# Useless TensorE products that stay on through the first attention block, three normalisations moved to POOL, and new costs for the weight splitting

## The chip, the cores and the metric

One core of one Trainium2 chip runs the whole program in one launch. The metric is device time in microseconds (us). Three runs of the kernel before took 1007.84, 1008.41 and 1009.18 us, so their median is 1008.41 us. Engines: PE (TensorE) multiplies matrices, DVE (VectorE), ACT (ScalarE) and POOL (GpSimd) work on elements, SP issues the DMAs.

## The reference, cut to what matters

```python
# attention: 4 x 8 heads x 768 tokens, head size 64, in windows of a chunk, its context and 8 memory tokens
scores = scale * np.matmul(q_c, k_full.transpose(0, 1, 3, 2))
a = np.exp(scores - np.max(scores, axis=-1, keepdims=True))
a = a / (np.sum(a, axis=-1, keepdims=True) + 1e-09)
out[:, :, c_start:c_end] = np.matmul(a, v_full)
...
# dense layer on 3072 tokens x 512
h = x @ w_in                                  # 512 -> 2048
x = np.maximum(0.01 * h, h) @ w_out           # 2048 -> 512
...
# 8 experts: each token goes to one, by the largest gate values, 384 tokens an expert
out[mask] = np.maximum(x[mask] @ w1[e], 0.0) @ w2[e]
```

## The kernel before

Work is cut into 32 groups of 96 queries (n in the code). Four groups make one block of 384 tokens (j); the dense layer then goes over a block in 16 steps (f), each with 128 columns of the hidden layer. Every product of the dense layer is made of three fp32r products, since each weight and each activation is held as a high and a low part (winh and winl, wouth and woutl, x1h and x1l, gh and gl).

A group of attention passes five stations. `scores` (L818) multiplies queries and keys into two PSUM banks; DVE takes scores, mask and row maximum (L822); ACT takes the exponentials (L827). `normalise` makes the reciprocal sums on DVE (L843, L845) and multiplies the 96x1024 exponentials by them (L847). `transpose` turns them on PE in two halves (L863), each into its own bank, and two copies bring them to SBUF as AT (L852 on ACT or L854 on DVE). `mix` multiplies by the values (L886) into one bank; that bank gives x1h (a cast on ACT or DVE) and x1l (a subtraction on DVE, L892).

The weights of the dense layer arrive as 64-bit numbers in 32 chunks, two for each step f (an input chunk and an output chunk). `weights` loads a chunk (L902, four buffers), scales its upper words on ACT (L909), puts the fp32 bits together on DVE in three passes (L910, L911, L913), casts the high part on ACT or POOL (L916, L917) and subtracts it on POOL for the low part (L918). This goes on beside the first block of the dense layer, until all chunks are split. `gemm1` (L934) and `gemm2` (L1027) of step f cannot start before their chunk.

The first block has no dense layer beside it. Its groups use other banks: the transposes of the first four groups go into po0 and po1, the mixed values into po2, which later gather `gemm2`; scores of the groups 1 and 3 use the two banks ph of `gemm1`.

The order of the instructions on each engine is set by a planner (`Plan`). Every piece of work is an `op` with the engines it may run on and a cost in us for each, a key and its dependencies; the planner plays through time with these costs and writes the instruction when it comes up. An engine runs its instructions in that order. A changed cost so moves work in later places too.

`keep_warm` plans a chain of useless products with the lowest priority: `warm` multiplies the identity by itself into columns 384 to 511 of a bank in the list `spots`, if one of them has not yet been taken over by later work; else it writes nothing. Nobody reads these columns. Before, the list holds the first buffer of po2 and one bank of the first group's scores.

Of the kernel before, what the change touches and what calls it, by code (L numbers as in the profile page):

```python
# [688 lines left out]
def kernel(ctx, tc, q, k, v, w, w_gate_t, we, out):  # L689
# [22 lines left out]
    S6 = SL * NF - ND  # L712
    EARLY = (S6 - 97.5) / 12
    PRE = 19
    NWARM, PAUSE, COLD = 60, 0.2, 8

    ctx.enter_context(tc.manual_schedule())
    P = Plan(nc)
# [83 lines left out]
    def scores(n):  # L802
        a = A[n]
        g = n % GB
        var = 0 if g == 0 else (2 if g == GB - 1 else 1)
        r = r_h if n < APB and n % 2 else r_a
        ps = [r.take() for _ in range(2)]
        X, st = a["X"], a["st"] = (r_ws if n == 2 else r_X).take(), r_st.take()
        if n == 2:
            X.view = lambda t: (t[:QB].rearrange("p a b -> p (a b)").bitcast(FT)  # L810
                                .rearrange("p (a b) -> p a b", a=H))
        a["e"] = []

        def mm():
            for i in range(KD):
                for r in range(2):
                    p = slice(64 * r, 64 * r + 64)
                    nc.tensor.matmul(ps[r].t[:QB, i * 128:(i + 1) * 128], a["q"][1]()[p, i, :], a["k"][1]()[p, i, :],  # L818
                                     start=True, stop=True)

        def mx(h):
            V.tensor_tensor_reduce(out=X.t[:, h, :], in0=ps[h % 2].t[:QB, h // 2 * 128:h // 2 * 128 + 128],  # L822
                                   in1=masks[:, var, :], scale=-scale, scalar=3.0e38, op0=OP.add, op1=OP.min,
                                   accum_out=st.t[:, 0, h:h + 1])

        def ex(h):
            S.activation(X.t[:, h, :], X.t[:, h, :], AF.Exp, bias=st.t[:, 0, h:h + 1], scale=-1.0,  # L827
                         accum_out=st.t[:, 2, h:h + 1])

        if n == 0:  # L830
            spots.append(ps[1])
        t = P.op(("T", 0.95), mm, [a["qd"], a["kd"]], [*ps, a["q"][0], a["k"][0]])
        for r in range(2):
            hs = slice(r, H, 2)
            for h in range(H)[hs]:
                o = P.op(("V", 0.215), lambda h=h: mx(h), [t], [ps[h % 2], X, st])
                a["e"].append(P.op(("S", 0.387), lambda h=h: ex(h), [o], [X, st]))

    def normalise(n):
        a = A[n]  # L840
        X, st = a["X"], a["st"]

        o = P.op(("V", 0.12), lambda: V.tensor_scalar(st.t[:, 3, :], st.t[:, 2, :], 1e-9, None, op0=OP.add),  # L843
                 [a["e"]], [st])
        o = P.op(("V", 0.12), lambda: V.reciprocal(st.t[:, 3, :], st.t[:, 3, :]), [o], [st])  # L845
        a["n"] = P.op({"V": 1.14} if n >= N1 or n < APB else {"V": 1.7, "G": 2.1},
                      lambda e=V if n >= N1 or n < APB else G: e.tensor_tensor(  # L847
            X.t, X.t, st.t[:, 3, :, None].to_broadcast([QB, H, 128]), op=OP.mult), [o], [X, st])

    def copy(e, out, x):  # L850
# [5 lines left out]
    def transpose(n):  # L856
        a = A[n]
        AT = a["AT"] = r_AT.take()
        a["t"] = []

        def tr(p, hh):
            for i in range(KD):
                nc.tensor.transpose(p.t[:, i * QB:(i + 1) * QB], a["X"].t[:, 4 * hh + i, :], ident[:QB, :QB])  # L863

        for hh in range(2):
            p = (r_o[hh] if n < APB else r_a).take()
            o = P.op(("T", 0.35), lambda p=p, hh=hh: tr(p, hh), [a["n"]], [p, a["X"]])
            a["t"].append(P.op({"S": 0.38, "V": 0.47} if n < APB else {"S": 0.38}, lambda e=S, p=p, hh=hh: copy(
                e, AT.t[:, 4 * hh:4 * hh + 4, :], p.t[:, :KD * QB].rearrange("p (a b) -> p a b", a=KD)),
                [o], [p, AT]))  # L870
# [3 lines left out]
    def mix(n):  # L874
        a = A.pop(n)
        j, u = divmod(n, APB)
        if u == 0:
            X1[j] = [r.take() for r in r_x1], []
        p = (r_o[2] if n < APB else r_a).take()
        sl = slice(u * QB, (u + 1) * QB)  # L880
        hi, lo = X1[j][0]

        def mm(hh):
            for h in range(4 * hh, 4 * hh + 4):
                i, r = divmod(h, 2)
                nc.tensor.matmul(p.t[64 * r:64 * r + 64, i * QB:(i + 1) * QB], a["v"].t[:, h, :], a["AT"].t[:, h, :],  # L886
                                 start=True, stop=True)

        pv = lambda: p.t[:, :KD * QB].rearrange("p (a b) -> p a b", a=KD)
        o = P.op(("T", 0.83), lambda: [mm(0), mm(1)], [a["t"], a["vd"]], [p, a["v"], a["AT"]])  # L890
        x = P.op({"S": 0.38, "V": 0.47} if n < APB else {"S": 0.38}, lambda e=S: copy(e, hi.t[:, :, sl], pv()), [o], [p, hi])
        y = P.op(("V", 0.47), lambda: V.tensor_tensor(lo.t[:, :, sl], pv(), hi.t[:, :, sl].bitcast(FT),  # L892
                                                      op=OP.subtract), [x], [p, hi, lo])
        X1[j][1].extend([x, y])
# [4 lines left out]
    def weights(c):  # L899
        f, half = divmod(c, 2)  # L900
        s, a, m, b = (r.take() for r in (r_ws, r_wa, r_wm, r_wp))
        d = P.dma(1.46, lambda: nc.sync.dma_start(s.t.rearrange("p a b -> p (a b)"),  # L902
                                                  w64[f][:, half * 1024:(half + 1) * 1024]), [], [s])

        hi, lo = (x[:, f, :] for x in (win if half == 0 else wout))
        mm = lambda: a.t.bitcast(FT)

        mi, lw, hw = (lambda: m.t.bitcast(I32)), (lambda: s.t[:, :, 0]), (lambda: s.t[:, :, 1])
        o = P.op(("S", 0.57), lambda: S.activation(m.t, hw().bitcast(FT), AF.Copy, scale=2.0 ** -112), [d], [s, m])  # L909
        o = P.op(("V", 0.45), lambda: V.tensor_scalar(b.t, mi(), 3, None, op0=OP.logical_shift_left), [o], [b, m])  # L910
        o = P.op(("V", 0.62), lambda: V.scalar_tensor_tensor(  # L911
            b.t, hw(), -0x80000000, b.t, op0=OP.bitwise_and, op1=OP.bitwise_or), [o], [s, b])
        o = P.op(("V", 0.62), lambda: V.scalar_tensor_tensor(  # L913
            a.t, lw(), 29, b.t, op0=OP.logical_shift_right, op1=OP.bitwise_or), [o], [s, a, b])
        x = P.op({"G": 0.7, "S": 0.54}, lambda e: (
            G.tensor_scalar(hi, mm(), 1.0, 0.0, op0=OP.mult, op1=OP.add) if e is G  # L916
            else S.activation(hi, mm(), AF.Copy)), [o], [a])  # L917
        y = P.op({"G": 1.3}, lambda e=G: e.tensor_tensor(lo, mm(), hi.bitcast(FT), op=OP.subtract),  # L918
                 [x], [a])
        WD[c] = [x, y]  # L920
# [156 lines left out]
            P.dep(o, [last], lat=pause if n > COLD else 0.0)  # L1077

    def warm():
        b = next((b for b in spots if not b.gone), None)  # L1080
        if b:
            nc.tensor.matmul(b.t[:, 384:], ident, ident, start=True, stop=True)

# [179 lines left out]
```

## Time and profile before

| what | us |
|---|---|
| median of three runs | 1008.41 |
| the profiled execution, its own time | 1008.72 |
| its span, first to last instruction | 1007.0 |
| PE busy in the span | 982.5 |
| DVE busy | 770.6 |
| ACT busy | 441.6 |
| POOL busy | 134.8 |

A line of the timeline gives the start, the duration, the engine, the line of the kernel, what is written from what, and the count; in brackets stands how long the engine had been idle and what it waited for. Matmuls overlap in the pipeline, so the distance from one start to the next is the better measure of what a group costs. The windows view gives the busy time of an engine in a stretch and the TensorE clock that was granted, as a share of 2.4 GHz: 1.00 is 2.4 GHz, 0.50 is 1.2 GHz.

### The profile page before, as it was taken

To read this page: it belongs to the slowest core of one execution; us is meant where nothing else is said; L and a number is where in the kernel's file an instruction comes from. 1 tells how busy PE (TensorE), PEld (TensorE's weight loads), DVE (VectorE), ACT (ScalarE), POOL (GpSimd) and SP (SyncE) were. 2 spreads that over 40 slices of the span, in tenths; PEclk is the share of its full clock that TensorE was granted. 3 is DMA by queue.
4 is the path that set the end of the run, shared out by engine and by line. 5 is a ranking of instruction groups with operands and counts; after the bars stand their busy time and mean duration, and the time that the engine had idled before them with its cause. 6 is when DMAs were issued, how large, how long until landed. Compare 5 with 4: busy or idle time off the path is not lost.

```text
span 1007.0 us, 17270 instructions
## 1 busy us (share of the span) xinstructions
PE 982.5 (98%) x6040; PEld 856.7 (85%) x6040; DVE 770.6 (77%) x2573; ACT 441.6 (44%) x1183; POOL 134.8 (13%) x149
## 2 busy tenths in 40 slices
PE   7999999999999999999999999999999999999997
PEld 6877888888988888888888889778888888888996
DVE  7989799698698599689689494588977888875720
ACT  7766634444444443544444324023434334334521
POOL 0767521000000000000000000010021112111211
PEclk9889999999999999999999999999999999999999
DMA  8656520021012111111210000044442624526600
GB/s 279 209 189 208 177 88 29 30 71 48 29 62 58 29 62 46 42 61 30 58 61 12 1 1 27 16 128 161 131 163 100 199 106 146 170 72 201 228 32 31
DMA packets 36326, 95.48 MB, mean 95 GB/s; under 512 B 4368, under 2 KB 8464, under 8 KB 36112
## 3 DMA queue, kind: packets, MB, share of 16 engines
q1 hardware_dynamic: 32400, 81.80, 25.3%
q0 software_dynamic: 3840, 12.59, 3.7%
q8 instruction: 47, 0.77, 0.3%
q14 instruction: 39, 0.32, 0.1%
HBM read 81.79 MB, written 12.58 MB: 94 GB/s over the span
## 4 chain that ended last, share of the span: by engine, by line
PE 81%; DVE 6%; issue 4%; DMA 3%; ACT 3%; POOL 2%; POOLq 0%; ACTq 0%; DVEq 0%; SPq 0%
PE po L1027 23%; PE ph L934 23%; PE ph L610 13%; PE po L633 11%; PE pa L818 2%; PE pa L886 2%; DVE junk L1057 2%; DMA wst<-in_w_dram 2%; PE pa L863 2%; PE pc L312 2%; ACT X L827 1%; DMA wgb<-in_w_gate_t_dram 1%; PE pt L479 1%; DVE wa L913 1%; DVE wp L911 1%
## 5 line engine op out<-in xcount | busy, mean ns | idle before, releaser
L1057 DVE CUSTOM_DVE_ANT_0 junk<-x,wgb 128x512 bf16<-128x512 f32 x296 | 207.8, 702 | 5.9 <-DMA wgb<-in_w_gate_t_dram 1.2
L942 ACT ACTIVATE gs<-ph 128x384 f32<-128x384 f32 x128 | 62.6, 489 | 195.2 <-PE ph L934 188.2
L1027 PE MATMUL po<-woutl,gh 128*128 128x512 f32 x336 | 134.5, 400 | 3.4 <-POOL woutl L918 3.4
L1027 PE MATMUL po<-wouth,gh 128*128 128x512 f32 x336 | 136.9, 407 | 0.0
L943 DVE TENSOR_TENSOR gs<-ph,gs 128x384 f32<-128x384 f32 x128 | 71.0, 555 | 85.0 <-ACT gs L942 84.5
L1027 PE MATMUL po<-wouth,gl 128*128 128x512 f32 x336 | 132.8, 398 | 1.2 <-POOL gl L945 1.2
L827 ACT ACTIVATE X<-X,st 96x128 f32<-96x128 f32 x248 | 97.0, 393 | 49.2 <-DVE st L822 49.0
L934 PE MATMUL ph<-x1h,winh 128*128 128x384 f32 x512 | 112.6, 342 | 1.2 <-ACT x1h L852 0.9
L934 PE MATMUL ph<-x1h,winl 128*128 128x384 f32 x512 | 111.0, 338 | 0.0
L934 PE MATMUL ph<-x1l,winh 128*128 128x384 f32 x512 | 110.3, 336 | 0.0
L934 PEld LDWEIGHTS ph<-x1h,winh 128*128 128x128 f32 x512 | 92.7, 190 | 11.6 <-POOL winh L916 1.2
L616 ACT ACTIVATE egh<-ph 128x384 fp32r<-128x384 f32 x64 | 31.4, 491 | 155.1 <-PE ph L610 151.0
L934 PEld LDWEIGHTS ph<-x1h,winl 128*128 128x128 f32 x512 | 93.0, 189 | 1.0
L934 PEld LDWEIGHTS ph<-x1l,winh 128*128 128x128 f32 x512 | 91.2, 189 | 0.3
L1027 PEld LDWEIGHTS po<-wouth,gl 128*128 128x128 f32 x336 | 63.4, 189 | 15.7 <-POOL gl L945 2.1
L1027 PEld LDWEIGHTS po<-woutl,gh 128*128 128x128 f32 x336 | 63.6, 189 | 14.9 <-POOL woutl L918 4.7
L1027 PEld LDWEIGHTS po<-wouth,gh 128*128 128x128 f32 x336 | 63.4, 189 | 13.9 <-ACT wouth L917 0.2
L944 ACT ACTIVATE gh<-gs 128x384 fp32r<-128x384 f32 x112 | 58.7, 524 | 36.5 <-DVE gs L943 36.3
L617 DVE SCALAR_TENSOR_TENSOR egl<-ph,egh 128x384 fp32r<-128x384 f32 x64 | 35.3, 552 | 45.1 <-ACT egh L616 44.8
L822 DVE CUSTOM_DVE_ANT_0 X<-pa,masks 96x128 f32<-96x128 f32 x232 | 56.7, 280 | 4.1 <-PE pa L818 4.1
L1142 POOL IOTA ij<- 128x128 int32 x1 | 0.2, 234 | 425.8 <-DVE L L1057 425.8
L945 DVE TENSOR_TENSOR gl<-gs,gh 128x384 fp32r<-128x384 f32 x88 | 48.5, 551 | 10.2 <-ACT gh L944 10.1
(243 smaller groups left out, 1932.0 us busy)
## 6 DMA issues: line engine op xcount, KB each, us to landing
west<-in_we_dram SPq DMA_DIRECT2D x56, 512.0 KB, 4.5
wst<-in_w_dram SPq DMA_DIRECT2D x32, 512.0 KB, 4.3
kt<-in_k_dram SPq DMA_DIRECT2D x31, 256.0 KB, 3.5
vt<-in_v_dram SPq DMA_DIRECT2D x30, 256.0 KB, 2.7
qt<-in_q_dram SPq DMA_DIRECT2D x31, 192.0 KB, 3.2
x2d<-x SPq DMA_DIRECT2D x21, 256.0 KB, 2.8
x<-in_we_dram SPq DMA_DIRECT2D x16, 256.0 KB, 3.0
wgb<-in_w_gate_t_dram SPq DMA_DIRECT2D x1, 2048.0 KB, 8.3
```

What stands on the lines that cost most here:

```text
L610: nc.tensor.matmul(ph.t[:, :TB], w[a].t[:, k * 128:(k + 1) * 128], xs[x].t[:, k, :], start=(n == 0), stop=(n == 3 * KD - 1))
L617: b = P.op(("V", 0.47), lambda: V.scalar_tensor_tensor(gl.t, ph.t[:, :TB], 0.0, gh.t.bitcast(FT), op0=OP.max, op1=OP.subtract), [a], [ph, ...
L633: nc.tensor.matmul(ACC[p][i].t, l.t[:, 128 * i:128 * i + 128], w[a].t[:, 512:1024], start=(f == 0 and n == 0), stop=(f == NF - 1 and n == 2))
L822: V.tensor_tensor_reduce(out=X.t[:, h, :], in0=ps[h % 2].t[:QB, h // 2 * 128:h // 2 * 128 + 128], in1=masks[:, var, :], scale=-scale, scal ...
L827: S.activation(X.t[:, h, :], X.t[:, h, :], AF.Exp, bias=st.t[:, 0, h:h + 1], scale=-1.0, accum_out=st.t[:, 2, h:h + 1])
L934: nc.tensor.matmul(ph.t[:, :TB], win[wt][:, f, kk * 128:(kk + 1) * 128], xt.t[:, kk, :], start=(n == 0 and kk == 0), stop=(n == 2 and kk = ...
L942: o = P.op(("S", 0.37), lambda: S.activation(t.t, ph.t[:, :TB], AF.Copy, scale=0.01), [o], [ph, t], key=k)
L943: o = P.op(("V", 0.47), lambda: V.tensor_tensor(t.t, ph.t[:, :TB], t.t, op=OP.max), [o], [ph, t], key=k)
L944: x = P.op(("S", 0.42), lambda: S.activation(gh(), t.t, AF.Copy), [o, gd], [t, *gb], key=k)
L945: y = P.op({"V": 0.47} if j > 1 else {"V": 0.47, "G": 0.96} if j else {"G": 0.96}, lambda e=V if j > 1 else G: e.tensor_tensor(gl(), t.t, ...
L1027: nc.tensor.matmul(acc.t, lt()[:, sl], wout[wt][:, f, :], start=(f == 0 and n == 0), stop=(n == 2 and (f == NF - 1 or s == S6 - 1)), skip_ ...
L1057: V.tensor_tensor_reduce(out=pools["wgb"].tile([128, DM], BF, name="junk"), in0=x, in1=WGB[0][:, e, :], scale=1.0, scalar=0.0, op0=OP.mult ...
```

## The change

It has three parts. The useless products may now go into the banks of the first four groups' transposes and mixed values, always the latest one that is in use, and up to 110 of them are planned where 60 were. The normalisation (L847) of the groups 0, 1 and 2 goes to POOL; that of group 3 stays on DVE. The planner's costs for the three bit passes on DVE and for the normalisations are raised.

```diff
-    NWARM, PAUSE, COLD = 60, 0.2, 8
+    NWARM, PAUSE, COLD = 110, 0.2, 8
...
-        if n == 0:
-            spots.append(ps[1])
...
-        a["n"] = P.op({"V": 1.14} if n >= N1 or n < APB else {"V": 1.7, "G": 2.1},
-                      lambda e=V if n >= N1 or n < APB else G: e.tensor_tensor(
+        eng = {"V": 1.2} if n >= N1 or n == APB - 1 else {"G": 2.1} if n < APB - 1 else {"V": 1.8, "G": 2.1}
+        a["n"] = P.op(eng, lambda e=V if n >= N1 or n == APB - 1 else G: e.tensor_tensor(
             X.t, X.t, st.t[:, 3, :, None].to_broadcast([QB, H, 128]), op=OP.mult), [o], [X, st])
...
             p = (r_o[hh] if n < APB else r_a).take()
+            if n < APB:
+                spots.append(p)
...
         p = (r_o[2] if n < APB else r_a).take()
+        if n < APB:
+            spots.append(p)
...
-        o = P.op(("V", 0.45), lambda: V.tensor_scalar(b.t, mi(), 3, None, op0=OP.logical_shift_left), [o], [b, m])
-        o = P.op(("V", 0.62), lambda: V.scalar_tensor_tensor(
+        o = P.op(("V", 0.62), lambda: V.tensor_scalar(b.t, mi(), 3, None, op0=OP.logical_shift_left), [o], [b, m])
+        o = P.op(("V", 0.64), lambda: V.scalar_tensor_tensor(
             b.t, hw(), -0x80000000, b.t, op0=OP.bitwise_and, op1=OP.bitwise_or), [o], [s, b])
-        o = P.op(("V", 0.62), lambda: V.scalar_tensor_tensor(
+        o = P.op(("V", 0.64), lambda: V.scalar_tensor_tensor(
             a.t, lw(), 29, b.t, op0=OP.logical_shift_right, op1=OP.bitwise_or), [o], [s, a, b])
...
-        b = next((b for b in spots if not b.gone), None)
+        b = next((b for b in spots[::-1] if (b.tile or b is spots[0]) and not b.gone), None)
```

Lines from L830 on stand up to two lower or higher in the changed file (L886 becomes L888, L934 L936, L1082 L1084, L847 L845, L918 L920).

PE, from the second half of group 1's transposes to the transposes of group 2. The names po with a number are buffers of the banks po0 to po2; in brackets stands the engine for whose earlier instruction a row waits. Before:

```order
L886 MATMUL po_346<-AT,vt 64x96 [waits DMAHW5_49,DVE_49,Activation_49]
L886 MATMUL po_346<-AT,vt 64x96 x3
L886 MATMUL po_346<-AT,vt 64x96 [waits Activation_49]
L886 MATMUL po_346<-AT,vt 64x96 x3
L863 MATMUL po_361<-ident,wst 128x96 [waits DVE_49,PE_49]
```

The same place now:

```order
L1084 MATMUL po_333<-ident 128x128 x2
L1084 MATMUL po_333<-ident 128x128 [waits Activation_49]
L888 MATMUL po_352<-AT,vt 64x96 [waits DMAHW5_49,DVE_49,PE_49]
L888 MATMUL po_352<-AT,vt 64x96 x7
L1084 MATMUL po_352<-ident 128x128
L1084 MATMUL po_352<-ident 128x128 [waits DVE_49]
L1084 MATMUL po_352<-ident 128x128
L1084 MATMUL po_352<-ident 128x128 [waits DVE_49]
L861 MATMUL po_387<-ident,wst 128x96 [waits PE_49,Pool_49]
```

Seven useless products now stand around the mix of group 1. Three of them wait: the first for ACT's copy of the bank po_333, the two others for DVE's cast and for DVE's subtraction from po_352. In turn these copies wait for the product ahead of them in the same bank.

PE, from the mix of group 3 to the first product of `gemm1`, now (before, `gemm1` followed the mix directly, and its third part waited for DVE):

```order
L888 MATMUL po_453<-AT,vt 64x96 x7
L1084 MATMUL po_453<-ident 128x128
L1084 MATMUL po_453<-ident 128x128 [waits DVE_49]
L1084 MATMUL po_453<-ident 128x128 x2
L1084 MATMUL po_453<-ident 128x128 [waits DVE_49]
L936 MATMUL ph<-x1h,winh 128x384 [waits Activation_49]
L936 MATMUL ph<-x1h,winh 128x384 x3
L936 MATMUL ph<-x1h,winl 128x384 [waits Pool_49]
```

The last product waits for DVE's subtraction x1l of group 3, and `gemm1` stands behind it. Five more products follow between the first steps of `gemm1`; 45 are written in all, where 21 were.

POOL, from its start of real work. Before:

```order
L916 TENSOR_SCALAR winh<-wa 128x512
L918 TENSOR_TENSOR winl<-wa,winh 128x512
L916 TENSOR_SCALAR winh<-wa 128x512
L918 TENSOR_TENSOR winl<-wa,winh 128x512
L918 TENSOR_TENSOR woutl<-wa,wouth 128x512
L916 TENSOR_SCALAR winh<-wa 128x512
L918 TENSOR_TENSOR winl<-wa,winh 128x512
L945 TENSOR_TENSOR gl<-gs,gh 128x384 x2
```

Now:

```order
L845 TENSOR_TENSOR X<-X,st 96x1024 x2
L845 TENSOR_TENSOR wst<-wst,st 96x1024
L920 TENSOR_TENSOR winl<-wa,winh 128x512 x2
L947 TENSOR_TENSOR gl<-gs,gh 128x384
L920 TENSOR_TENSOR woutl<-wa,wouth 128x512
L918 TENSOR_SCALAR winh<-wa 128x512
L920 TENSOR_TENSOR winl<-wa,winh 128x512
L947 TENSOR_TENSOR gl<-gs,gh 128x384
```

The three normalisations stand first on POOL, and the casts of the first two input chunks have left it (they are on ACT). On DVE the three normalisations of 96x1024 are gone from the first block; two copies AT and three casts x1h that ACT had done stand there now, and the first three bit passes come after them. In the attention that follows, the transposes and the mix of a group stand up to one step f earlier on PE than before; the routing and expert stages have the same work in a slightly other order.

## Rows read from the trace of the kernel before

**Rows 1.** The page: span, and PE busy us (share) and instructions.
```profile
span 1007.0 us, 17270 instructions
...
PE 982.5 (98%) x6040; PEld 856.7 (85%) x6040; DVE 770.6 (77%) x2573; ACT 441.6 (44%) x1183; POOL 134.8 (13%) x149
```
**Rows 2.** Windows, PE alone: stretch, length, PE busy (x), granted clock, DMA share, GB/s.
```profile
20.00:24.00 4.00, 1.04 (x17) 0.93 0.84 277
...
60.00:64.00 4.00, 4.00 (x21) 0.50 0.76 230
...
96.00:100.00 4.00, 2.39 (x14) 1.00 0.51 166
```
**Rows 3.** Timeline of PE, end of the first block and first steps of gemm1.
```profile
21.28 0.97 PE L886 MATMUL po<-AT,ve 128*64 128x96 f32 x16 [1.21 <-ACT X L827]
25.04 1.51 PE L863 MATMUL po<-ident,X 96*128 96x96 f32 x8 [2.79 <-DVE X L847]
...
28.93 1.62 PE L934 MATMUL ph<-x1h,winh 128*128 128x384 f32 x4 [0.89 <-ACT x1h L852]
...
33.98 0.85 PE L934 MATMUL ph<-x1h,winl 128*128 128x384 f32 x4
34.67 0.85 PE L934 MATMUL ph<-x1l,winh 128*128 128x384 f32 x4
```
**Rows 4.** Timeline of PE, steps 3 to 6 of the first dense block.
```profile
50.84 0.39 PE L1027 MATMUL po<-wouth,gh 128*128 128x512 f32 x1
...
55.07 0.50 PE L1027 MATMUL po<-wouth,gh 128*128 128x512 f32 x1
57.91 0.80 PE L1027 MATMUL po<-woutl,gh 128*128 128x512 f32 x1 [2.34 <-POOL woutl L918]
...
64.44 0.97 PE L934 MATMUL ph<-x1h,winh 128*128 128x384 f32 x4
...
67.77 0.50 PE L1027 MATMUL po<-wouth,gh 128*128 128x512 f32 x1
```
**Rows 5.** Timeline of POOL: low parts of weights and of g.
```profile
28.35 1.27 POOL L918 TENSOR_TENSOR winl<-wa,winh 128x512 fp32r<-128x512 f32 x1
...
54.58 1.01 POOL L945 TENSOR_TENSOR gl<-gs,gh 128x384 fp32r<-128x384 f32 x1 [2.28 <-ACT gh L944]
55.55 2.31 POOL L918 TENSOR_TENSOR woutl<-wa,wouth 128x512 fp32r<-128x512 f32 x1
```
**Rows 6.** Timeline of DVE: a copy, x1l, third bit passes, a normalisation.
```profile
13.58 1.01 DVE L854 COPY AT<-po 128x384 f32<-128x384 f32 x2
...
16.79 0.56 DVE L892 TENSOR_TENSOR x1l<-po,x1h 128x384 fp32r<-128x384 f32 x1 [0.30 <-ACT x1h L852]
...
22.44 0.68 DVE L913 SCALAR_TENSOR_TENSOR wa<-wst,wp 128x512 int32<-128x512 int32 x1
...
32.21 0.67 DVE L913 SCALAR_TENSOR_TENSOR wa<-wst,wp 128x512 int32<-128x512 int32 x1
...
55.52 1.21 DVE L847 TENSOR_TENSOR X<-X,st 96x1024 f32<-96x1024 f32 x1
...
114.77 0.68 DVE L913 SCALAR_TENSOR_TENSOR wa<-wst,wp 128x512 int32<-128x512 int32 x1
```
**Rows 7.** Timeline of PE, first half of the first block: products, transposes, mix.
```profile
6.99 0.94 PE L1082 MATMUL po<-ident 128*128 128x128 f32 x6
7.85 1.12 PE L818 MATMUL ph<-kt,qt 64*96 64x128 f32 x16
...
12.72 0.88 PE L863 MATMUL po<-ident,X 96*128 96x96 f32 x8
13.44 0.86 PE L1082 MATMUL po<-ident 128*128 128x128 f32 x6
14.36 0.88 PE L886 MATMUL po<-AT,vt 128*64 128x96 f32 x16
```
**Rows 8.** Timeline of ACT: the first exponential of group 2.
```profile
13.59 0.39 ACT L827 ACTIVATE wst<-wst,st 96x128 f32<-96x128 f32 x1
```

## The prediction

> **What bounds the kernel now.** The page comes first: PE is busy 982.5 of 1007.0 us [rows 1], so from the end of weight splitting on, time is PE's, and what PE loses or gains earlier is carried to the end. The windows view shows where PE is not at its best: in 20 to 24 us it is busy 1.04 us and its clock has begun to fall, in 60 to 64 it is busy throughout at 0.50 [rows 2]. There are two such spells.
>
> The first lies at the end of the first attention block. PE waits 1.21 us for ACT, then 2.79 us for the normalisation of group 3 on DVE; the transposes at 25.04 then take 1.51 us, the clock has dropped to 1.2 GHz, and `gemm1` starts at 28.93 [rows 3]. Its first four quarters of four matmuls take 33.98 - 28.93 = 5.05 us; at full clock a quarter takes 34.67 - 33.98 = 0.69, so four would take 2.76.
>
> The second lies in step 4 of `gemm2`. PE stops for 2.34 us because POOL delivers woutl late, and goes on at half clock until about 64.4 [rows 4]. Why POOL is late stands in its own timeline: woutl stood behind a gl that had waited for ACT, and then took 2.31 us where such a subtraction else takes 1.27 [rows 5], since it ran beside DVE's normalisation of group 5 (55.52, [rows 6]). What this spell costs: from 50.84 to 67.77 PE did two steps of `gemm2` and `gemm1`, one group's transposes and mix and one group's scores. A step of both takes 55.07 - 50.84 = 4.23 [rows 4]; two are 8.46, with about 0.72 + 0.85 + 1.1 for the three others [rows 7] 11.1. The stretch took 16.93, so 5.8 were lost.
>
> Between the two and up to 115 us DVE's bit passes run nearly without rest: the third pass of the first chunk starts at 22.44, of the fourth at 32.21, of the last at 114.77 [rows 6], 2.95 us a chunk from the fourth on. DVE and PE need about the same time for a step here, so neither can run far ahead of the other.
>
> **The change, part by part.** *Useless products.* Three take 7.85 - 6.99 = 0.86 us [rows 7], 0.29 each. As work they cost PE little in the first block, since they lie in its waits. But they are not free for others: the rows of the new order on PE show products that wait for the reading of the bank into which they write, and copies that wait for the product ahead.
>
> The Trainium skill speaks against writing there without such waits: "PSUM — Partial Sum Buffer", section "PSUM bank collisions raise a hardware error", says that two engines may not be in one bank and quadrant at once, even in different columns, and that PSUM is to be guarded by bank. No trace of before shows it, since there no product stands in a bank that is being read. By products that hinder nobody, `gemm1` would start 2 to 2.5 us earlier than I put it below; I take the waits as the new order shows them.
>
> *POOL's normalisations.* The trace has none on POOL. POOL takes 1.01 us for 384 columns and 1.27 for 512 [rows 5], 2.0 ns a column and 0.2 fixed, so about 2.3 to 2.4 for 1024; DVE takes 1.21. The lower bound is DVE's 1.21, the upper twice POOL's slowed 2.31, 4.6. I take 2.4: in these stretches DVE mostly reads PSUM, and the slowed row stands beside a DVE operation on two SBUF operands. The Trainium skill ("GPSIMD Engine Reference", section 3.1) measured 4497 ns for 2048 fp32 columns; half of it, 2.25, is an estimate for 1024 and would move the sum by some 0.2.
>
> *The chain of the first block, new.* Group 2's exponentials begin at 13.59 [rows 8], so group 1's end there; with two small DVE operations POOL starts group 1 at 14.2 and ends at 16.6. Transposes take 13.44 - 12.72 = 0.72 [rows 7]: 17.4. Two products (0.58) stand before ACT's copy, which ends at 18.5; a third waits for it; mix (0.8 to 0.9, [rows 7]) ends at 19.7. Then product, DVE's cast (0.5, as one of the two copies in 1.01), two products, x1l (0.5), product: 22.3. Only now come group 2's transposes, though POOL had done with it at 20.9. They end at 23.0; product, product, DVE copy: 24.2; group 3's normalisation on DVE: 25.4. Group 2's mix with its products ends at 26.0, group 3's transposes at 26.7, product, copy and product at 27.9, mix at 28.7, product and cast at 29.6, three products at 30.6, x1l at 31.2, product at 31.6. There `gemm1` starts, **2.7 us later** than at 28.93. With POOL at 1.21 the same chain gives about 31.0, with 4.6 some 35.
>
> *The clock.* Both falls came after a wait of over 2 us (2.79 and 2.34, [rows 3, 4]); from 96 to 100, where PE's shorter waits add up to 4.00 - 2.39 = 1.61 us, the clock stayed at 1.00 [rows 2]. In the new block PE's gaps are all 0.7 us or shorter, so I take it that it holds: **5.05 - 2.76 = 2.3 less**. Five products stand on PE between `gemm1` and `gemm2`: 5 x 0.29 = **1.45 more**. PE is so 2.7 - 2.3 + 1.45 = **1.85 us late** when the first block's own work is done.
>
> *DVE.* Three normalisations leave (3.65), two copies and three casts come (2.5), 1.15 less. But it now waits for PE's handovers some 3 us, and the first bit passes come later: by the same chain the first chunk's third pass starts at 27.1 for 22.44, the fourth's at 37.0 for 32.21. A normalisation and a maximum (1.75) that followed the fourth now precede it, so DVE is about 3 us behind in like work. The raised costs by themselves add no work. DMAs of the chunks are issued when a third pass frees a buffer, so 3 to 5 us later as well, with the same four buffers in the ring.
>
> *The second spell.* In the new order group 5's transposes and mix stand one step earlier. With PE 1.85 late, `gemm2` of step 3 begins at about 52.5. DVE comes to group 5's normalisation at about 51.2, again beside POOL's woutl, which ends at 53.5: 0.9 us of waiting. In step 5 winl stands on POOL behind a gl that waits for ACT: 0.8 more. Such gaps are shorter than that of before, the clock should not fall. So 5.8 lost become 1.7: **4.1 us less**. DVE, which had waited 2.6 us in that spell for PE's mix, then does not, and is back level with before by the 16th chunk.
>
> Afterwards all is as before: the later waits of PE and the rest of the program follow in like order. The moved rows of the routing and expert stages are the same work; I take nothing for them, an estimate of 1 either way.
>
> Sum: 1.85 - 4.1 = **-2.25 us**. The profiled execution took 1008.72 (span 1007.0, 1.7 around it), 0.3 more than the median of 1008.41; from the median the forecast is **1006.2**, a span of 1004.7 in an execution like the profiled one.
>
> **The rivals.** *The second spell stays (slower).* If POOL's woutl comes as late for PE as before (2.3 us) at the group 5 place, the clock falls there again and the 5.8 us are paid as before; with DVE 3 us behind and PE only 1.85, the wait is even 1.15 longer. Then 1.85 + 1.15 remain: 1011.4. For it: POOL's order still has gl ahead of each low part. Against: the transposes moved ahead by a step, so that DVE reaches the normalisation with fewer chunks behind it.
>
> *The weights set the pace.* DVE, 3 us behind after the first block, keeps PE waiting in many small places up to the last chunk: 3 us less the 2.6 of DVE's own wait in the old spell leaves 0.4, some 1008.8, no change. For it: 2.95 us a chunk, twice a step, is more than PE's 4.23. Against: DVE had idle time in that pace.
>
> *The clock falls in the first block all the same (slower).* The products keep the gaps short, but there are a dozen of them. Then the 2.3 are not won, and from 24 us on the chain's PE work, about 7 us, is nearly doubled in part: 5 more, so 1.85 + 2.3 + 5 - 4.1 = 5, 1013.5.
>
> *POOL at 4.6.* 3.5 later: 1009.7, a change that measurement hardly tells.
>
> **How the numbers follow.** Forecast 0.43, the weights' pace 0.24, the second spell 0.17, the clock 0.08, slow POOL 0.05, the rest 0.03 for gains beyond the forecast. Measurements of this kernel tell about 0.2%, 2 us, from no change. The forecast case is itself near that bound (-2.2); its small waits may vanish (to -3.9, and with the later waits of PE 1002.5) or grow, so a fifth of it counts as no change, and a part of the weights' case as faster. Faster 0.43, same 0.29, slower 0.28. The range from 1002.8 to 1012.0 leaves out the fallen clock above and a gain past every wait below.
>
> **What the profile after would show.** Right: a granted clock of 1.00 from 16 to 36 us; `gemm1` starting at 31 to 32 with quarters of 0.69; products between; POOL's L847 near 2.4; no PE gap over 1.5 us up to 70 and clock 1.00 from 56 to 64; the last L913 at 112 to 116. Wrong: 0.50 anywhere before 36 or near 56; a first `gemm1` before 30 or after 33; POOL over 3 us; new waits in the routing stage, after 600 us.

## The result and the profile after

The changed kernel took a median of 1013.32 us (1011.84 to 1017.76, 7 runs) beside 1008.45 (1007.84 to 1009.18) of the kernel before: a ratio of 1.0056, with a 95% interval of 1.0039 to 1.0074. It is slower by about 5 us; 2 us faster was forecast.

The page of the changed kernel (the lines that answer to [rows 1]):

```profile
span 1011.1 us, 17363 instructions
...
PE 986.2 (98%) x6088; PEld 860.0 (85%) x6088; DVE 770.0 (76%) x2575; ACT 442.8 (44%) x1185; POOL 135.7 (13%) x145
```

The span is 4.1 us longer and PE is busy 3.7 us more. Where these arise is read by one step's place in both traces. ACT's evacuations of `gemm1` (before's line 942) start between 0.6 and 7.0 us late up to 160 us, then 1.7 us late at nearly every step from 171 to 631 us, the whole rest of the dense layer. The first evacuation of the experts (line 616) comes 5.6 late, the last one 4.1. So 1.7 us were lost before 171 us, and 2.4 net between 631 and the end, in the routing and expert stages. This split is that of one execution: in four other profiles with the same order up to 631 us, shown below, the 1.7 is 0.6, 2.5, 3.6 and 6.3.

The first block went as forecast. PE's timeline of the changed kernel (answers to [rows 3]; line 1084 is the useless product, 936 `gemm1`):

```profile
18.03 0.49 PE L1084 MATMUL po<-ident 128*128 128x128 f32 x2 [0.78 <-ACT AT L850]
...
20.40 0.71 PE L1084 MATMUL po<-ident 128*128 128x128 f32 x4 [0.65 <-DVE x1h L852]
21.76 0.49 PE L1084 MATMUL po<-ident 128*128 128x128 f32 x2 [0.65 <-DVE x1l L894]
...
24.03 0.71 PE L1084 MATMUL po<-ident 128*128 128x128 f32 x4 [0.65 <-DVE AT L852]
...
31.66 0.96 PE L936 MATMUL ph<-x1h,winh 128*128 128x384 f32 x4
32.46 0.86 PE L936 MATMUL ph<-x1h,winl 128*128 128x384 f32 x4
...
48.65 0.50 PE L1029 MATMUL po<-wouth,gh 128*128 128x512 f32 x1
...
67.29 0.39 PE L1029 MATMUL po<-wouth,gh 128*128 128x512 f32 x1
...
71.81 0.50 PE L1029 MATMUL po<-wouth,gh 128*128 128x512 f32 x1 [0.18 <-ACT wouth L919]
73.66 0.51 PE L1029 MATMUL po<-woutl,gh 128*128 128x512 f32 x1 [1.34 <-POOL woutl L920]
...
97.44 0.50 PE L1029 MATMUL po<-woutl,gh 128*128 128x512 f32 x1 [1.35 <-POOL woutl L920]
...
103.00 0.50 PE L1029 MATMUL po<-woutl,gh 128*128 128x512 f32 x1 [1.11 <-POOL woutl L920]
...
691.84 0.33 PE L348 MATMUL pc<-g,ones 128*128 128x384 bf16 x1
694.18 0.18 PE L377 MATMUL pc<-ex,tri 128*128 128x1 bf16 x1 [2.01 <-DVE need L370]
...
695.00 1.26 PE L610 MATMUL ph<-xth,winl 128*128 128x384 f32 x4
```

Nearly every handover shows the same picture: the product is what waits, for the engine that reads the bank. `gemm1` starts at 31.66 and its quarters take 0.7 to 0.8. At 48.65 and 67.29 `gemm2` of the steps 2 and 5 begins. The rows behind are places where PE lost time that the forecast did not have: woutl in the steps 6, 10 and 11 (73.66, 97.44, 103.00), and in the routing stage line 377, behind which the first expert's products (line 610) run slowly. The windows view of PE (answers to [rows 2]; the fifth and sixth rows hold step 6, the last one line 377):

```profile
20.00:24.00 4.00, 2.33 (x18) 1.00 0.27 93
24.00:28.00 4.00, 3.39 (x36) 1.00 0.65 199
28.00:32.00 4.00, 2.70 (x28) 1.00 0.57 199
60.00:64.00 4.00, 3.98 (x30) 1.00 0.58 190
72.00:76.00 4.00, 2.66 (x7) 0.75 0.56 179
76.00:80.00 4.00, 4.00 (x21) 0.82 0.36 132
96.00:100.00 4.00, 2.65 (x13) 1.00 0.53 184
695.00:700.00 5.00, 5.00 (x22) 0.66 0.42 111
```

Both old falls of the clock are gone, and there are two new ones. DVE's third bit passes (line 915, answers to [rows 6]: the first, fourth, 16th and last of 32), and its longest wait between the last two of them:

```profile
27.01 0.68 DVE L915 SCALAR_TENSOR_TENSOR wa<-wst,wp 128x512 int32<-128x512 int32 x1
...
37.70 0.69 DVE L915 SCALAR_TENSOR_TENSOR wa<-wst,wp 128x512 int32<-128x512 int32 x1
...
71.32 0.68 DVE L915 SCALAR_TENSOR_TENSOR wa<-wst,wp 128x512 int32<-128x512 int32 x1
...
80.04 0.56 DVE L945 TENSOR_TENSOR gs<-ph,gs 128x384 f32<-128x384 f32 x1 [1.41 <-ACT gs L944]
...
118.50 0.68 DVE L915 SCALAR_TENSOR_TENSOR wa<-wst,wp 128x512 int32<-128x512 int32 x1
```

The four passes stand at 22.44, 32.21, 70.31 and 114.77 before: 4.6, 5.5, 1.0 and 3.7 late. On POOL (answers to [rows 5]) a normalisation takes 1.89, and the gl ahead of the late woutl starts 1.98 after POOL's last work; ACT, which makes its gh, had waited 1.00 until 70.16 for a chunk of weights from DMA:

```profile
10.93 1.89 POOL L845 TENSOR_TENSOR X<-X,st 96x1024 f32<-96x1024 f32 x1 [9.85 <-DVE st L822]
...
71.37 1.01 POOL L947 TENSOR_TENSOR gl<-gs,gh 128x384 fp32r<-128x384 f32 x1 [1.98 <-issue]
72.34 1.26 POOL L920 TENSOR_TENSOR woutl<-wa,wouth 128x512 fp32r<-128x512 f32 x1
```

### The profile page after: what moved, and what is told of

It is laid out like the page before. It is cut to its first block, busy times and chain, and to the rows that moved or that the text cites. A ratio compares the mean times of both kernels' runs of the same rounds, so it can differ in the third digit from the quotient of the medians.

```text
span 1011.1 us, 17363 instructions
## 1 busy us (share of the span) xinstructions
PE 986.2 (98%) x6088; PEld 860.0 (85%) x6088; DVE 770.0 (76%) x2575; ACT 442.8 (44%) x1185; POOL 135.7 (13%) x145
## 4 chain that ended last, share of the span: by engine, by line
PE 87%; issue 4%; DMA 2%; POOL 2%; DVE 2%; ACT 2%; POOLq 0%; ACTq 0%; SPq 0%; DVEq 0%
PE po L1029 26%; PE ph L936 24%; PE ph L610 13%; PE po L633 12%; PE pa L818 3%; PE pa L888 2%; DMA wst<-in_w_dram 2%; PE pa L861 2%; PE pc L312 2%; PE po L1084 1%; PE pt L479 1%; ACT X L827 1%; POOL woutl L920 1%; DMA xg<-x2d,idx 1%; POOL out_dram L650 0%
## 5 line engine op out<-in xcount | busy, mean ns | idle before, releaser
L936 PE MATMUL ph<-x1h,winh 128*128 128x384 f32 x512 | 111.7, 340 | 0.3 <-DVE gs L945 0.3
L936 PE MATMUL ph<-x1h,winl 128*128 128x384 f32 x512 | 110.7, 337 | 0.1
L936 PE MATMUL ph<-x1l,winh 128*128 128x384 f32 x512 | 109.7, 335 | 0.0
L936 PEld LDWEIGHTS ph<-x1h,winh 128*128 128x128 f32 x512 | 92.0, 189 | 10.3 <-DVE gs L945 0.8
L936 PEld LDWEIGHTS ph<-x1h,winl 128*128 128x128 f32 x512 | 92.2, 188 | 1.8 <-POOL winl L920 1.0
L936 PEld LDWEIGHTS ph<-x1l,winh 128*128 128x128 f32 x512 | 90.6, 188 | 0.3
```

Source lines behind the costliest of these rows:

```text
L936: nc.tensor.matmul(ph.t[:, :TB], win[wt][:, f, kk * 128:(kk + 1) * 128], xt.t[:, kk, :], start=(n == 0 and kk == 0), stop=(n == 2 and kk = ...
```

## The experiments

Theory: the loss has two places. The products in banks that are handed over make DVE late, and the end of weight splitting follows DVE; and the planner, whose times the change shifts, writes another order of the routing stage. The main rivals: that all comes from the late front, that any product costs wherever it stands, or that the fallen clock is the loss.

The planner's count of products (`NWARM`) sets the later order apart from the front: planned products for which no bank is left emit no instruction, but take planned time. So the two places can be exchanged. "Front" is the order up to the end of weight splitting.

| kernel | front's order | products | later order | median us | ratio to before (95%) |
|---|---|---|---|---|---|
| front only | change | 45, handed-over banks | before's, 7 places off | 1010.75 | 1.0026 (1.0010 to 1.0041) |
| front only again | same | same | same | 1010.74 | 1.0033 (1.0016 to 1.0049) |
| later only | before | 21 | change's, 7 places off | 1009.83 | 1.0021 (1.0007 to 1.0035) |
| no bank products | change | 20 | before's, 7 places off | 1007.30 | 0.9991 (0.9974 to 1.0008) |
| products only | before | 45, handed-over banks | before | 1011.08 | 1.0028 (1.0012 to 1.0044) |
| free products | change | 38, free bank | before's, 7 places off | 1005.74 | 0.9994 (0.9979 to 1.0008) |
| before, free | before | 39, free bank | before | 1009.25 | 1.0017 (0.9999 to 1.0035) |
| normalisations only | own | as before | before | 1005.92 | 1.0001 (0.9984 to 1.0017) |
| costs only | own | as before | before | 1004.78 | 0.9970 (0.9954 to 0.9986) |
| costs, free | costs only's | 37, free bank | before | 1002.18 | 0.9949 (0.9932 to 0.9966) |
| change, free bank | change | 38, free bank | change | 1008.16 | 1.0007 (0.9990 to 1.0024) |
| change again | change | 45, handed-over banks | change | 1014.30 | 1.0070 (1.0043 to 1.0098) |
| change a third time | change | same | change | 1012.28 | 1.0053 (1.0034 to 1.0073) |
| later covered | before | 21 | 140 places off | 1008.61 | 1.0007 (0.9987 to 1.0026) |

The kernel before had medians of 1008.58, 1007.17, 1007.78 and 1007.85 beside them, in 23 to 35 runs each, all but one of which lie within 8.0 to 9.5 us of each other; so ratios are compared, not medians of different rows. The quotient of two medians differs from the ratio by up to 0.0013 (1005.92 by 1007.17 is 0.9988, where the table has 1.0001).

**Front only, and later only.** The change with `NWARM` 60, and before with `NWARM` 90:

```diff
-    NWARM, PAUSE, COLD = 110, 0.2, 8
+    NWARM, PAUSE, COLD = 60, 0.2, 8
```

```diff
-    NWARM, PAUSE, COLD = 60, 0.2, 8
+    NWARM, PAUSE, COLD = 90, 0.2, 8
```

> The changed kernel with one number set back (60 planned products in place of 110). All 45 products in the first block stay, and so does the order of everything up to the end of weight splitting; the later order of routing and experts falls back to that of before, but for 7 small places. Theory 'two places': of the 4.1 us that the profiled execution lost, 1.7 stand at the end of weight splitting and the rest in the later order. Then this kernel keeps the 1.7 alone: about 1010.1 us, between 1009.4 and 1010.8, with the first routing products near 670 us level with before but for 1.7. Rival 'all from the front': the later order is harmless in itself, and the waits after 670 us come from what the front pushes later (buffers, transfers). Then it stays near the changed kernel's 1013.3.

> The kernel before with one number raised (90 planned products in place of 60; the same 21 are executed). Its order up to the end of weight splitting is that of before without any difference, the later order is that of the changed kernel but for 7 small places. Theory 'two places': slower by what the later order costs, 2.4 to 3.9 us, so 1010.9 to 1012.3, with a wait of about 2 us before the product on ex (source line 377) and a stretch of half clock behind it. Rival 'all from the front': level with before, 1008.4.

The front-only profile is 2.5 us late from 171 to 631 us and 2.1 at the end; later only is 0.3 early there and 2.0 late at the end. Each is slower by itself, later only by less than expected (1009.83 for 1010.9 to 1012.3), and the excesses add to 1.0047 (with 1.0033 to 1.0054), near the change's 1.0053 to 1.0070. The rival that the later order is harmless falls. The later-only kernel has the wait and the half clock where the change has them; PE's timeline:

```profile
689.73 0.33 PE L348 MATMUL pc<-g,ones 128*128 128x384 bf16 x1
692.07 0.18 PE L377 MATMUL pc<-ex,tri 128*128 128x1 bf16 x1 [2.01 <-DVE need L370]
...
693.15 1.49 PE L610 MATMUL ph<-xth,winl 128*128 128x384 f32 x4
```

A group of four takes 1.3 us there from start to start, where it else takes 0.7.

**No products between the handovers, and products only.** The first is the change with the old places of the products (the diff below, `NWARM` 60 and the old choice of a bank), the second before with the new places alone:

```diff
+        if n == 0:
+            spots.append(ps[1])
...
-            if n < APB:
-                spots.append(p)
...
-        if n < APB:
-            spots.append(p)
```

> POOL's three normalisations and the new planner costs as in the changed kernel, but the useless products stand where they stood before (20 of them, none in the first block's banks between its handovers); later order as before but for 7 small places. So it differs from the front-only kernel by the products alone. Theory from the forecast's own terms: gemm1 starts about 2 us earlier than 31.66, the clock falls again and the first quarters pay 2.3, the five products on PE (1.45) are gone: 1 to 1.5 us less than the front-only kernel, near 1008.8. Rival 'the products pay': gaps without products let the clock fall for longer, the clock costs 5 us and more, and it is slower than the front-only kernel, 1012 or above.

> The kernel before with the useless products in the first block's banks (45 executed in place of 21) and nothing else: the order of all other work is that of before without a difference, up to the end. Theory from the forecast's terms: the clock holds, 2.3 us less; the waits of the products and of the copies behind them lengthen the chain by 2 to 2.5, and some products more on PE cost about 1: level to 1.5 slower, 1008.4 to 1010. Rival 'the weights set the pace': what the front gains or loses up to 36 us is given back by 130 us, level with before, 1008.4 within 0.5. If the second spell near 56 us vanishes with it, 1004 to 1006.

The products are what costs: with the change's front 3.5 us (0.9991 to 1.0026), with before's 2.8. Both go the way of the forecast's own terms, and further. Without them the clock is 0.66, 0.50 and 0.56 in the three windows from 20 to 32, and `gemm1` still starts at 28.08 and DVE's last third pass at 114.6, where front only has 32.54 and 119.1. So a held clock bought less than the waits cost.

**A bank that nobody reads.** Is it the products, or the banks? Here they go on in the second bank of group 3's scores, after its last maximum, which clears `busy`:

```diff
+            if h == H - 1:
+                ps[1].busy = False
...
-        if n == 0:
+        if n in (0, APB - 1):
             spots.append(ps[1])
+            ps[1].busy = n > 0
...
-        b = next((b for b in spots if not b.gone), None)
+        b = next((b for b in spots if not b.gone and not getattr(b, "busy", False)), None)
```

> As the kernel with POOL's normalisations and the new costs and no products between the handovers (1007.30 us), but 18 of 38 useless products now go on through the first block in a bank that nobody reads or waits for: that of group 3's scores, after its last maximum and until gemm1's second step. Theory 'handover waits': the products cost only because they stand in banks that are handed over, so here they cost nothing and hold the clock: the transposes and mixes after 20 us at full clock, gemm1 at 26 to 27.5 in place of 28.08, its first four quarters in 2.8 in place of 5.1; what DVE's pace to the last bit pass (114.6) leaves of that is open, so 1004.5 to 1007.3. Rival 'any product costs': the products themselves, by their place on PE, push the chain; then 1009 to 1010.75, like the front-only kernel.

> The kernel before with the useless products going on in the same bank that nobody reads (39 in place of 21), nothing else moved. It stands against the products-only kernel (45 in the handed-over banks, 1011.08). Theory 'handover waits': level with before or up to 2.3 us faster, 1006.3 to 1008.6, with gemm1 at 27 to 28.5 and its quarters at 0.69. Rival 'any product costs': 1010 to 1011.

> The changed kernel in full, its planner numbers and both its orders, with one difference: the products that go on through the first block (38 in all, for 45) stand in the bank that nobody reads, not in the banks that are handed over. Theory 'two places add': the handed-over banks cost what the front-only kernel showed against its counterpart (ratios to before 1.0026 against 0.9994), the later order what the later-only kernel showed (1.0021): so 0.9994 + 0.0021 = 1.0015 here, some 1.5 us above before and some 4 us below the changed kernel run beside it. Rival 'the later order costs only behind a late front': level with the kernel of free products, 0.9994. Rival 'the bank is not the cause': as the changed kernel, 1.0045 or more.

In the change's front the bank is the cause: with 38 products in place of 45 and all else the same, 1.0007 for the free bank against 1.0070 for the handed-over ones on the same chip, and 0.9994 against 1.0026 with before's later order. PE's timeline of the change with the free bank (line 1085 is the product) shows transposes, mixes and `gemm1` following without the 0.65 us waits, and `gemm1` at 26.50 in place of 31.66:

```profile
18.08 1.16 PE L1085 MATMUL ph<-ident 128*128 128x128 f32 x8
19.35 0.88 PE L866 MATMUL po<-ident,wst 96*128 96x96 f32 x8
20.07 1.08 PE L1085 MATMUL ph<-ident 128*128 128x128 f32 x8
21.29 1.01 PE L889 MATMUL po<-AT,ve 128*64 128x96 f32 x16
...
26.50 0.95 PE L937 MATMUL ph<-x1h,winh 128*128 128x384 f32 x4
```

With before's front the two banks are not told apart (1.0017 and 1.0028, with overlapping intervals), and 1009.25 missed the 1006.3 to 1008.6 of the theory. And with the change's front the held clock gave nothing that can be told: free products 0.9994 (the profile holds 1.00 from 20 to 32), none 0.9991, by whose intervals up to 2 us are possible. Whether the later order costs as much behind this early front is open too: the interval of 1.0007 holds both 1.0015 and 0.9994.

**What sets the end of the front.** Thirteen of the profiles answer it, those that have one of the two fronts. From DVE's last third pass to ACT's 41st evacuation of `gemm1` it is 123.5 to 123.8 us in the five kernels with before's front, and 121.2 to 121.8 in the eight profiles with the change's front, while the last third pass itself lies anywhere from 112.4 to 123.0. Three rows, of the changed kernel, of the change with the free bank and of the change again (the last passes of the latter two start at 112.41 and 123.00):

```profile
240.08 0.49 ACT L944 ACTIVATE gs<-ph 128x384 f32<-128x384 f32 x1 [2.54 <-PE ph L936]
```

```profile
233.88 0.49 ACT L945 ACTIVATE gs<-ph 128x384 f32<-128x384 f32 x1 [2.54 <-PE ph L937]
```

```profile
244.74 0.49 ACT L944 ACTIVATE gs<-ph 128x384 f32<-128x384 f32 x1 [2.54 <-PE ph L936]
```

240.08 - 118.50, 233.88 - 112.41 and 244.74 - 123.00 are 121.6, 121.5 and 121.7. So a wait of PE up to 115 us counts only as far as the last pass comes later by it. Which of the two engines leads up to there is not shown by this: between the first and the last third pass DVE stands still for 6.6 us of 93.0 before and 7.9 of 92.2 after, PE for 8.1 and 8.3, and each waits for the other's work. The change's order itself is worth some 2 us behind the last pass (123.64 before, 121.58 after): PE is busy throughout from 120 to 160, where it stood for 1.2 us before.

**One part alone.**

> The kernel before with POOL normalising the first three groups, the old planner costs and the old products; the later order is that of before without a difference. The three parts without products gave 1.3 us less. If that gain is DVE's relief of three normalisations (3.65 us of DVE work out of its first 18 us), it is here: 1006.5 to 1007.5. If it comes from the new costs' order after 36 us, this one is level with before or slower by what POOL's 1.89 us a group add to the chain (0.7 a group): 1008 to 1009.5.

> The kernel before with the new planner costs of the three bit operations alone (the costs of the normalisations stay old); the later order is that of before without a difference, the front's order differs in 23 to 26 places. If the gain of the kernel without products comes from the planned order (transposes and mixes a step earlier in the weights stage), it is here: 1006.5 to 1007.5. Rival: the order alone changes nothing, since DVE's 2.95 us a chunk sets the pace whatever the order: 1008.4 within 0.7.

```diff
-        a["n"] = P.op({"V": 1.14} if n >= N1 or n < APB else {"V": 1.7, "G": 2.1},
+        eng = {"V": 1.14} if n >= N1 or n == APB - 1 else {"G": 2.1} if n < APB - 1 else {"V": 1.7, "G": 2.1}
...
-        o = P.op(("V", 0.45), lambda: V.tensor_scalar(b.t, mi(), 3, None, op0=OP.logical_shift_left), [o], [b, m])
+        o = P.op(("V", 0.62), lambda: V.tensor_scalar(b.t, mi(), 3, None, op0=OP.logical_shift_left), [o], [b, m])
...
```

POOL's normalisations alone are level (the profiled execution is the fastest of its runs, so its last pass at 112.1 says little). The new costs of the bit operations alone are faster by 3 us, more than either side expected: the last third pass starts at 110.4, 4.3 earlier than before. PE's timeline shows where that arises. From the start of `gemm2` in step 2 to that in step 5 PE does the same work in before, costs only and the change; before takes 67.77 - 46.66 = 21.1 us, costs only 63.14 - 46.32 = 16.8, the change 67.29 - 48.65 = 18.6. The first row is from before, the other two from costs only:

```profile
46.66 0.39 PE L1027 MATMUL po<-wouth,gh 128*128 128x512 f32 x1
```

```profile
46.32 0.39 PE L1027 MATMUL po<-wouth,gh 128*128 128x512 f32 x1
...
63.14 0.39 PE L1027 MATMUL po<-wouth,gh 128*128 128x512 f32 x1
```

Here PE waits 0.35 and 0.26 us on woutl in place of 2.34, and the clock stays at 1.00. With POOL's normalisations beside the new costs, also without products in the banks, woutl is late in the steps 2, 3, 6, 7, 10 and 11, by 0.85 to 1.51 us each, and the ratio is 0.9991 for 0.9970; the intervals overlap.

> The kernel with the new costs of the bit operations alone (ratio 0.9970, the fastest so far) and products in the bank that nobody reads. Theory 'the last bit pass sets the end of the front': the clock held in the first block gives nothing, as it gave nothing with the other two orders (0.9994 against 0.9991, 1.0017 against 1): 0.9970 within 0.0012. Rival 'the clock's 2.3 us are time': 0.9947.

This is the fastest kernel of the study. The point lies at the rival's 0.9947, but the interval reaches into that of costs only: whether the held clock is worth 2 us here stays open.

**The change once more.**

> The changed kernel once more, on the same chip as the others, since it was so far measured in seven runs that spread over 6 us. By the sum of the two places (1.0026 and 1.0021) 1.0047; by its first measurement 1.0056 (1.0039 to 1.0074).

Its profiled execution spans 1014.6 us, and shows what that of the first measurement had escaped. PE's timeline, then its windows:

```profile
21.66 0.49 PE L1084 MATMUL po<-ident 128*128 128x128 f32 x2 [0.65 <-DVE x1l L894]
...
24.45 1.22 PE L1084 MATMUL po<-ident 128*128 128x128 f32 x4 [0.65 <-DVE AT L852]
25.60 1.55 PE L888 MATMUL po<-AT,ve 128*64 128x96 f32 x16
...
35.06 1.63 PE L936 MATMUL ph<-x1h,winh 128*128 128x384 f32 x4
```

```profile
20.00:24.00 4.00, 2.85 (x18) 0.82 0.28 100
24.00:28.00 4.00, 3.55 (x25) 0.50 0.33 124
28.00:32.00 4.00, 3.31 (x30) 0.82 0.54 182
32.00:36.00 4.00, 2.80 (x11) 0.60 0.28 84
```

The waits are the same as in the first profile up to the fall, 0.65 and 0.78 each, and the clock fell all the same. `gemm1` starts at 35.06, and ACT's evacuations are 6.3 us late after 171 us.

> The front-only kernel a second time. Up to 670 us its instructions are the changed kernel's, row for row, and yet the mean granted clock fell below 0.994 in none of its 12 runs and in 7 of the 17 runs of the changed kernel (0.989 to 0.992 there, 1015.6 to 1019.2 us). 'The fall is chance, and the same for both': some of these runs show 0.991 or less and 1013 to 1017 us, and the two kernels run side by side differ by the later order alone, 1.2 to 2.4 us. 'The later order brings the fall about': the changed kernel again 3.5 to 4.4 us above this one, with no low clock here.

> The changed kernel a third time, beside the front-only kernel on the same chip. 'Chance': its median is 1.2 to 2.4 us above that of the front-only kernel, and low clocks come in both or in neither. 'The later order brings the fall about': 3.5 to 4.4 us above, low clocks here alone.

A mean granted clock of 0.992 or less came in 9 of 29 runs of the change and in 1 of 24 runs of the front-only kernel. Side by side the two differ by 1.5 us in the median and 0.0020 in the ratio, as "chance" had it; but 3 against 1 low clocks in 12 runs each are too few to say that they are as frequent in both. All the change's runs with 0.994 or less took 1015.6 to 1019.2 us, the others 1010.3 to 1014.6. Only one fall in the first block was seen in a profile; where the others' clock fell is open. The profile of front only again is 0.6 us late from 171 to 631 us, that of the change a third time 3.6, both with a clock of 1.00 from 20 to 40.

**The routing stage covered.** Before with `NWARM` 80:

> The kernel before with 80 planned products in place of 60: order up to the end of weight splitting as before without a difference, 21 executed; the later order differs from that of before in 140 places, but behind the product on g (source line 348) there stand again 13 matmuls of the first expert ahead of the product on ex (line 377); in the later-only kernel there was none. Theory 'the uncovered product': the 2 us of waiting at line 377 and the half clock behind it are the later loss, so this one is level with before, 1.0000 within 0.0010. Rival 'moved rows cost by themselves': 1.0015 to 1.0030.

The moved rows cost little as such: 1.0007, with an interval that holds 1, but 1.0021 too. In the profiles the later part is 0.6 us longer than before's here, and 2.3 in later only. PE's timeline shows why; line 377 finds PE at work:

```profile
689.96 0.96 PE L610 MATMUL ph<-xth,winh 128*128 128x384 f32 x4 [0.20 <-ACT xth L482]
...
692.15 0.34 PE L610 MATMUL ph<-xth,winh 128*128 128x384 f32 x1
692.51 0.18 PE L377 MATMUL pc<-ex,tri 128*128 128x1 bf16 x1
```

With the uncovered line 377 the later part costs 2.1 to 2.4 us in the three profiles in which the clock fell behind it (0.66 to 0.76 in a window of 5 us), and 1.2 to 1.3 in the two in which it held. In the profiles with before's later order, and those 7 places off, the same part differs from before's by -0.6 to 1.5, so only the first three stand out.

## Why the prediction was wrong

**The step that failed** is the second spell's: "So 5.8 lost become 1.7: **4.1 us less**", with "DVE [...] is back level with before by the 16th chunk. Afterwards all is as before". Up to the spell the sum held: `gemm2` of step 2 starts at 48.65 for 46.66, 2.0 us late, where 1.85 was put. From there to step 5 PE needs 18.6 us for 21.1: **2.5 us are won, not 4.1**, and 3.3 stay lost in place of 1.7. The clock held at 1.00; the waits on woutl are 0.85 and 1.37 where 0.9 and 0.8 were put, and the rest was not taken apart. PE stands 0.5 us early behind it, where the forecast had 2.25; DVE's 16th third pass is 1.0 late.

**The larger part failed behind that place.** "Afterwards all is as before" became 4.2 us of loss on PE: `gemm2` of step 16 starts 3.7 late, DVE's last third pass 3.7, outside the 112 to 116 given. woutl is late in the steps 6, 10 and 11, where before has one such wait, 1.03 in step 11. Behind the first of them the clock falls, so `gemm1` is slow, and DVE stands still for its evacuation (1.41 at 80.04); between its 16th and its last third pass DVE stands for 4.2 us, where it stood for 1.2. Behind the last pass the new order is 2 us shorter: 3.7 becomes the +1.7 in place of -2.25. How much of the 3.7 is the fallen clock at 72 to 80 is bounded by the front-only kernel's second profile: the same front, the same wait of 1.35 in step 6, a clock of 1.00, and a last pass at 117.39, 1.1 earlier.

The late woutl belong to the new order, not to the late start. All eight profiles with the change's front have them in the steps 2, 3, 6 and 10, the change with the free bank too, whose `gemm1` starts 5.2 us earlier (0.86, 1.22, 1.35 and 1.00); of the five with before's front none has. One of its rows:

```profile
68.66 0.50 PE L1030 MATMUL po<-woutl,gh 128*128 128x512 f32 x1 [1.35 <-POOL woutl L921]
```

What the handed-over banks cost comes on top, and is carried along whole. Between the change with the free bank and front only again, one front and a clock of 1.00 from 16 to 120 us in both, `gemm1` stands 5.1 us apart, step 5 4.6, the last third pass 5.0, the 41st evacuation 5.1. With the free bank that evacuation is 4.5 us earlier than before (in a profile that is the fastest of its runs), with the handed-over banks 0.6 later.

**The rival "The weights set the pace"** came nearest: small waits in many places up to the last chunk. It had the size wrong: "3 us less the 2.6 of DVE's own wait in the old spell leaves 0.4". DVE's own new waits took the place of the 2.6. That DVE's lateness makes PE wait, as it says, is not shown, since the waits on woutl are there behind an early front as well.

**The moved rows of the routing and expert stages**, "I take nothing for them, an estimate of 1 either way", cost 2.4 us in the profiled execution, and 0.0021 in a kernel of their own. No row of this stage stands ahead of the prediction. In the trace of before 17 products of the first expert stand between line 348 and line 377, whose operand DVE works out from the result of the former (2.34 us from start to start in the change, 694.18 - 691.84); the new order puts line 377 ahead of all of them. That could be seen in the order, and was not costed.

**The useless products.** The chain was right to 0.1 us (31.6, measured 31.66), in part by luck: in three other profiles of this front with a held clock `gemm1` starts at 31.64, 32.54 and 33.23, and POOL's 2.4 was 1.89. But "By products that hinder nobody, `gemm1` would start 2 to 2.5 us earlier than I put it" undersized what the handovers cost: 26.50 and 27.36 were measured, 4.3 to 5.2 earlier. The Trainium skill ("PSUM — Partial Sum Buffer", section "PSUM bank collisions raise a hardware error") asks to guard PSUM by bank; the trace shows what such guards took here, waits of 0.58 to 0.78 us before the products at the handovers, and no run here leaves them out.

**The clock**: "I take it that it holds" was right for the first profile and not for the change's second. The rival that the clock falls all the same, at 0.08 and 1013.5, came true in that execution, and may have in the other runs of 1015.6 us and more. That 1013.5 also lies at the first measured median of 1013.32 is luck: the profiled execution of 1012.88 held the clock in the first block. "Such gaps are shorter than that of before, the clock should not fall" held for the two waits it meant (0.85 and 1.37); behind the one of 1.34 us in step 6 the clock was 0.75 in the stretch from 72 to 76, and behind 1.35 in step 10 it was 1.00. Held, the clock gave nothing that can be told with the change's order, where 2.3 were counted.

## What to carry to other kernels

A wait that vanishes is a gain only if no other comes up behind it: price the new order over the whole stage, between the same two pieces of work, and not over one spell. Filler work belongs into a bank that nobody is about to read, since in one that is handed over it can turn each handover into a wait for both sides; with the change's front that cost more than the held clock could bring. When a planner writes the order, a change of its costs or counts at one end moves rows hundreds of microseconds later: price each chain of small dependent steps there by the work that still stands between its links.

## What was not expected of the hardware

The same waits of PE, 0.65 to 0.78 us each in the same order, went with a granted clock of 1.00 in one execution and 0.50 in another; and behind the wait on woutl in step 6, 1.23 to 1.36 us in the five profiles with the handed-over banks, it fell in two. One small DVE operation on 96x8 (line 841, 0.16 in the median of its 32) took 1.02 us at 74.56 in the changed kernel, while POOL ran a low part of the weights beside it.
